# Attention and two MLPs in full precision: the ninth score block and its maxima, one bank for a head's sums, a 5/4 split of the subtraction, and new order numbers

## The chip, the cores and the metric

The kernel runs on one core of a Trainium2 chip. The metric is device time in microseconds (us) of one execution. TensorE (PE) multiplies, VectorE (DVE), ScalarE (ACT) and GpSimd (POOL) work elementwise, and SyncE (SP) issues all DMAs. Each of them works through its own list of instructions in order; they wait for each other on semaphores.

## The reference

Everything is fp32. Batch 2, 8 heads, 1152 keys, head size 64; two queries are averaged into one, so that each head has 576 queries. The attention output (1152 x 512) goes through two MLPs of width 2048.

```python
q_pool = q.reshape(B, H, S // 2, 2, D).mean(axis=3)
scores = scale * np.matmul(q_pool, k.transpose(0, 1, 3, 2))
scores = scores - np.max(scores, axis=-1, keepdims=True)
attn = np.exp(scores)
attn = attn / (np.sum(attn, axis=-1, keepdims=True) + 1e-09)
out = np.matmul(attn, v)
# x: the heads side by side, 1152 x 512
h = x @ w_in;  g = softplus(h);        x = g @ w_out      # first MLP
h = x @ w_in2; g = P(h) / (Q(h) + 1e-06); x = g @ w_out2  # second MLP, P and Q polynomials
```

## The kernel before

**What sets the order.** Nothing is issued where it is written. Each piece of work is an operation in a `Plan` (lines 62 to 194): its engine, a guessed duration, what it reads and writes, and a priority `at`. A list scheduler (`order`, line 130) then picks operation after operation by its guessed start times and by the priorities, gives out the buffers of the SBUF arena and of the eight PSUM banks, and the kernel issues the result (line 857). The priorities come from two tables of numbers, `OFF` for the attention and `OFF2` for the MLPs (lines 197 to 255), times a unit time T. The result is one fixed list for each engine. Which semaphore waits stand in it is decided afterwards by what the instructions touch.

**Attention, one head** (`head`, line 400). SP loads K, Q and V. POOL averages the query pairs (L423). PE transposes K and Q (L438, L450), ACT and DVE copy the transposes out of PSUM (L333 and L335 are the copy helper). A head is then worked off in two *units*, the two column halves of 288 queries (`hf` 0 and 1); 16 heads make 32 units, here numbered 0 to 31, so that even units are first halves. A score matrix stands with the keys on the partitions: nine blocks of 128 keys x 288 queries.

**One unit** (`unit`, line 471). PE computes the blocks in pairs into one of two PSUM buffers of two banks (L560, `sc`); block 8, which has no partner, is computed as two pieces of 144 columns, and it is the first of the unit (line 474). ACT copies each pair into the SBUF buffer `st` (L333, 128x576). DVE takes the running maximum over the blocks (L479): three operations over 576 columns with one input in PSUM, and two over 288 columns with both inputs in SBUF (lines 488 and 491: one brings in block 8 from `st`, one joins the two halves of the running maximum). PE transposes the maximum (L496), DVE reduces it (L500), PE spreads it over all partitions into a bank `mB` (L506), and ACT copies `mB` to SBUF (L512) for POOL. DVE subtracts the maximum from blocks 0 to 5 (L582, 128x1728, with `mB` in PSUM), POOL from blocks 6 to 8 (L582, 128x864, with the copy); ACT takes the exponential of each part (L589). The split is `ND = 6` (line 359).

**Values and sums** (`values`, line 517). PE multiplies the unit's nine blocks by V (L527, 64 rows, two blocks at a time in the two column halves of the array) and by a column of ones (L527, 1 row, four at a time in four quarters of the array) for the sums. Each unit has its own sum bank, its own copy of it by ACT (97x288) and its own four small DMAs (L545) that bring the four partial sums to 32 partitions. `norm` (line 595) adds them on POOL (L600, L603), takes the reciprocal on DVE (L605), sends it through DRAM (L607, L610) and multiplies on POOL (L616); each second head is then split into two fp32r parts `xh` and `xl` on POOL (L337, L348).

**The MLPs** (`moe`, line 645) multiply in fp32r, each product as three matmuls of high and low parts (L706, L788), with the weights converted by DVE (L664, L667, L670) and split by ACT and POOL. Some of the weight conversions stand between the attention's operations.

In the rows, `banks` is PSUM as a whole, `arena` and `arena_r` are the two large SBUF buffers.

Of the kernel before, what the change touches and what calls it, by code (L numbers as in the profile page):

```python
# [8 lines left out]
F32 = mybir.dt.float32  # L9
# [8 lines left out]
class Slot:  # L18


    def __init__(self, mem, off, size):
        self.mem, self.off, self.size = mem, off, size
        self.occ, self.over, self.lower = None, [], []

# [37 lines left out]
class Plan:  # L62
# [13 lines left out]
    def kind(self, name, phase, mem, offs, size, fifo=True):  # L76
        self.kinds[name] = Kind(name, phase, [Slot(mem, o, size) for o in offs], fifo)
# [52 lines left out]
    def order(self, slack, wait, stick):  # L130
        slots = [(kd, sl) for kd in self.kinds.values() for sl in kd.slots]
        for kd, sl in slots:
            for kx, x in slots:
                if x.mem is sl.mem and x.off < sl.off + sl.size and sl.off < x.off + x.size:
# [8 lines left out]
        while len(done) < len(self.ops):  # L143
            best = None
            for eng, l in cand.items():
# [15 lines left out]
                rank = lambda x: (x[1].prio + (abs(stick) if eng == "P" and x[1].mode != mode else 0.0), x[1].seq)  # L161
# [36 lines left out]
    'ld': 557.737,  # L198
    'tk': -3.506,
    'tke': -1199.93,  # L200
    'sq': 766.784,
    'tq': -1.626,
    'tqe': -1539.22,
    'lv': 734.191,
    'sc': -32.575,
    'ev': 2600.14,
    'mx': -558.886,
    'mt': -1059.58,
    'mr': -2884.99,
    'mb': -250.221,  # L210
    'sh': 2069.22,
    'ex': -278.049,
    'stick': 237.605,
    'ms': 872.18,
    'shg': 287.226,
    'exg': 898.812,
    'sm': 21.776,
    'so': -1632.41,
    'pv': 22.561,
    'pvs': -7.928,  # L220
    'po': -1438.22,
    'nm': 1549,
}
OFF2 = {
    'ld': -443.752,
    'hi': 746.06,
    'lo': -1233.92,
    'sp': 253.133,
    'ld2': -559.421,
    '1a': 1580.59,  # L230
    '1d': 171.246,
    '1y': 449.295,
    '1r': -443.221,
    '1z': -878.321,
    '1g': -600.605,
    'gh': 601.506,
    'gl': 330.365,
    '2h': -60.264,
    '2a': 372.297,
    '2t': -364.801,  # L240
    '2q': -994.888,
    '2b': 446.759,
    '2A': 737.678,
    '2m': 1387.29,
    '2n': 217.018,
    '2r': 386.142,
    '2g': -648.914,
    'out': 215.416,
    'end': 2687.08,
    'c1': -10155.3,  # L250
    'c2': -10450.6,
    'co': 13.248,
    's0': -557.188,
    's1': 1876.07,
# [7 lines left out]
WAIT = 0.088  # L262
SLACK = 0.009
# [27 lines left out]
def fused_kernel(  # L291
# [35 lines left out]
    ones = const.tile([128, 1], F32, name="ones")  # L327
# [31 lines left out]
    ND = 6  # L359
# [15 lines left out]
    def lay_ps(phase, **what):  # L375
        for name, (bs, n) in what.items():
# [5 lines left out]
             ("mp", 2, 2304), ("mb", 2, 1152), ("mc", 2, 32), ("dc", 2, 288), ("rc", 2, 72))  # L382
# [13 lines left out]
    def attention():  # L396
# [3 lines left out]
        def head(hd):  # L400
# [64 lines left out]
            dc = P.buf("dc", [32, 2, 4, HW // 32], F32)  # L465
            for hf in range(2):
                st = unit(hd, hf, kx, qT)
                values(hd, hf, st, vf, ud, dc, t0 + hf * T)
# [48 lines left out]
        def values(hd, hf, st, vf, ud, dc, t0):  # L517
            pv = P.buf("pv", [128, HW], F32)
            sm = P.buf("sm", [128, HW], F32)

            def tiles(out, lhs, m, c, n):
# [367 lines left out]
```

## Time and profile before

| | us |
|---|---|
| three runs: median (lowest to highest) | 730.65 (724.06 to 731.75) |
| the profiled execution, its own time | 729.63 |
| span of its instructions | 727.8 |

| engine | busy us | share of the span |
|---|---|---|
| PE | 682.6 | 94% |
| DVE | 582.3 | 80% |
| ACT | 540.5 | 74% |
| POOL | 505.2 | 69% |

The profile shows one execution. A group of instructions has a line of the kernel, an engine, what it writes and reads, and the mean of one in ns. Matmuls overlap, and their ends are modelled: a PE that reads as busy is not at its limit. The chain is the work that ended last, followed back from the end, so it tells which engine the time stood on.

### The profile page before, as it was taken

What the parts mean: (1) busy time and instruction counts of PE and PEld (TensorE: products, weight loads), DVE (VectorE), ACT (ScalarE), POOL (GpSimd) and SP (SyncE); (2) the same over time, 40 slices, a digit from 0 to 9 for tenths busy, and PEclk for the clock granted to TensorE, in tenths of its full rate; (3) what the DMA queues carried; (4) which work ended last, traced back from release to release, by engine and by line L of the source; (5) the groups of instructions that cost most, each with busy time, mean ns of one, the idle gap of its engine ahead of it and who ended that gap; (6) DMA issues with size and microseconds to landing.
All of it is one profiled execution on the core that took longest, in us unless ns stands there. A gap on an engine that the chain in (4) does not pass through costs nothing.

```text
span 727.8 us, 13061 instructions
## 1 busy us (share of the span) xinstructions
PE 682.6 (94%) x4612; PEld 530.4 (73%) x4612; DVE 582.3 (80%) x761; ACT 540.5 (74%) x1027; POOL 505.2 (69%) x513
## 2 busy tenths in 40 slices
PE   7998888879989889999999999999989999999997
PEld 5443444435444445569999999999978899898996
DVE  4787989767777789975325789999999988879796
ACT  3776677757767767796777887778887889986773
POOL 2443656444645554689767997879999889998673
PEclk9999999989999999999999999999999999999999
DMA  6222322212222224335102358788813011110011
GB/s 206 56 74 79 91 72 69 70 27 58 61 61 61 61 55 120 105 110 169 31 1 87 91 181 297 271 280 277 270 44 102 30 56 46 52 37 30 16 45 43
DMA packets 57457, 70.77 MB, mean 97 GB/s; under 512 B 13232, under 2 KB 38832, under 8 KB 57392
## 3 DMA queue, kind: packets, MB, share of 16 engines
q1 hardware_dynamic: 57392, 69.94, 31.4%
q8 instruction: 36, 0.59, 0.3%
q14 instruction: 29, 0.24, 0.1%
HBM read 58.99 MB, written 10.78 MB: 96 GB/s over the span
## 4 chain that ended last, share of the span: by engine, by line
PE 55%; DVE 19%; ACT 9%; POOL 6%; issue 5%; DMA 4%; SPq 1%; DVEq 0%; POOLq 0%; ACTq 0%
PE banks L706 21%; PE banks L788 20%; DVE arena L479 10%; PE banks L560 5%; PE banks L527 5%; ACT arena L333 4%; DVE arena L582 3%; ACT arena L589 1%; DVE banks L770 1%; POOL arena_r L348 1%; PE banks L496 1%; POOL arena L348 1%; DMA arena<-in_moe_w_out_dram 1%; POOL arena L766 1%; ACT arena_r L333 1%
## 5 line engine op out<-in xcount | busy, mean ns | idle before, releaser
L706 PE MATMUL banks<-xh,arena_r 128*128 128x384 f32 x768 | 212.3, 338 | 4.1 <-DVE arena_r L348 3.5
L788 PE MATMUL banks<-arena_r 128*128 128x384 f32 (+1 forms) x1008 | 214.0, 360 | 1.1 <-DVE arena_r L348 0.8
L333 ACT COPY arena<-banks 128x576 f32<-128x576 f32 (+5 forms) x309 | 147.2, 515 | 81.6 <-PE banks L560 35.1
L788 PEld LDWEIGHTS banks<-arena_r 128*128 128x128 f32 x1008 | 181.5, 188 | 16.2 <-POOL arena_r L348 1.3
L706 PEld LDWEIGHTS banks<-xh,arena_r 128*128 128x128 f32 x768 | 140.4, 188 | 10.5 <-DVE arena_r L348 7.4
L706 PE MATMUL banks<-xl,arena_r 128*128 128x384 f32 x384 | 129.3, 337 | 0.0
L770 DVE RECIPROCAL banks<-arena 128x384 f32<-128x384 f32 x48 | 122.6, 2554 | 6.7 <-POOL arena L762 5.4
L582 POOL TENSOR_TENSOR arena<-arena 128x864 f32<-128x864 f32 x32 | 65.8, 2057 | 82.8 <-ACT arena L333 82.7
L560 PE MATMUL banks<-arena 64*128 64x288 f32 (+1 forms) x640 | 104.3, 428 | 14.2 <-DVE arena L479 8.4
L348 POOL TENSOR_TENSOR arena<-arena 128x384 f32<-128x384 f32 x96 | 97.6, 1022 | 17.6 <-ACT arena L740 11.9
L348 POOL TENSOR_TENSOR arena_r<-arena,arena_r 128x512 fp32r<-128x512 f32 x64 | 82.5, 1299 | 18.8 <-ACT arena_r L333 18.6
L479 DVE TENSOR_TENSOR arena<-banks,arena 128x576 f32<-128x576 f32 x96 | 72.4, 754 | 28.2 <-ACT arena L333 23.3
L589 ACT ACTIVATE arena<-arena 128x864 f32<-128x864 f32 (+1 forms) x64 | 81.3, 1289 | 8.5 <-DVE arena L582 5.1
L560 PEld LDWEIGHTS banks<-arena 64*128 64x128 f32 x640 | 52.3, 191 | 45.4 <-DVE arena L479 15.3
L527 PE MATMUL banks<-arena 128*64 128x288 f32 (+1 forms) x640 | 83.8, 394 | 0.0
L348 DVE TENSOR_TENSOR arena_r<-banks,arena_r 128x384 fp32r<-128x384 f32 x96 | 52.8, 550 | 31.9 <-ACT arena_r L333 31.4
L706 PEld LDWEIGHTS banks<-xl,arena_r 128*128 128x128 f32 x384 | 72.1, 188 | 1.4
L333 ACT CAST arena_r<-banks 128x384 fp32r<-128x384 f32 x96 | 46.2, 481 | 26.1 <-DVE banks L771 12.1
L527 PEld LDWEIGHTS banks<-arena 128*64 128x64 f32 x640 | 40.7, 136 | 34.0 <-issue 10.2
L582 DVE TENSOR_TENSOR arena<-arena,banks 128x1728 f32<-128x1728 f32 x32 | 61.9, 1935 | 3.7 <-PE banks L506 2.9
L762 POOL TENSOR_TENSOR arena<-arena 128x384 f32<-128x384 f32 x48 | 49.0, 1021 | 22.3 <-ACT arena L756 22.1
L756 ACT ACTIVATE arena<-banks,par 128x384 f32<-128x384 f32 x96 | 63.8, 684 | 0.0
(54 smaller groups left out, 953.7 us busy)
## 6 DMA issues: line engine op xcount, KB each, us to landing
arena<-in_moe_w_in_dram SPq DMA_DIRECT2D x32, 512.0 KB, 4.3
arena<-in_moe_w_out_dram SPq DMA_DIRECT2D x32, 512.0 KB, 4.0
sp<-arena SPq DMA_DIRECT2D x32, 256.0 KB, 3.4
arena<-sp SPq DMA_DIRECT2D x32, 256.0 KB, 3.0
arena<-in_k_dram SPq DMA_DIRECT2D x16, 288.0 KB, 3.0
arena<-in_q_dram SPq DMA_DIRECT2D x16, 288.0 KB, 3.2
arena<-in_v_dram SPq DMA_DIRECT2D x16, 288.0 KB, 3.0
arena<-rr SPq DMA_DIRECT2D x16, 144.0 KB, 3.0
```

The source lines that it names most:

```text
L333: nc.scalar.copy(o, i)
L348: e.tensor_tensor(out=o, in0=a, in1=b, op=ALU.subtract)
L479: P.op("V", dve_t(m * HW), lambda: nc.vector.tensor_tensor(out=o(), in0=x(), in1=y(), op=ALU.max), r=r, w=w, at=t0 + (OFF['mx'] + 0.15 * j ...
L527: nc.tensor.matmul(out=out()[r:r + m, o:o + w], lhsT=lhs(x), rhs=st()[:, x, o:o + w], start=(c == 0), stop=(c == KC - 1), skip_group_check ...
L560: nc.tensor.matmul(out=ps()[:, i, 0:w], lhsT=kx()[D * i:D * i + D, j, :], rhs=qT()[D * i:D * i + D, q0:q0 + w], start=True, stop=True,)
L582: (nc.vector, nc.gpsimd)[g].tensor_tensor(out=s, in0=s, in1=mB()[:, None, :].to_broadcast([128, n, HW]), op=ALU.subtract)
L589: nc.scalar.activation(out=s, in_=s, func=AF.Exp, scale=escale)
L706: nc.tensor.matmul(out=hp(), lhsT=w()[:, kk * 128:(kk + 1) * 128], rhs=x[:, kk, :], start=(kk == 0 and n == 0), stop=(kk == KD - 1 and n = ...
L756: return lambda: nc.scalar.activation(out=o(), in_=i(), func=AF.Identity, scale=sc, bias=bi)
L762: P.op("G", pool_t(CW), lambda: nc.gpsimd.tensor_tensor(out=Q(), in0=t(), in1=ah(), op=ALU.add), r=[t, ah], w=[Q], at=a("2q"))
L770: P.op("V", (69 + 6.25 * CW) / 1e3, lambda: nc.vector.reciprocal(out=h(), in_=Q()), r=[Q], w=[h], at=a("2r"))
L788: nc.tensor.matmul(out=o()[:, 0:w_], lhsT=lt, rhs=rh, start=(f == 0 and n == 0), stop=(f == FG - 1 and n == 2),)
```

## The change

1. Block 8 is computed last in a unit instead of first. Its maximum is read from its PSUM bank: DVE takes the maximum of block 8's two pieces with one half of the running maximum, writes the result into free columns of block 8's own bank, and then joins that with the other half. Both operations over 288 columns now have one input in PSUM and one in SBUF.
2. `ND = 5`: DVE subtracts from five blocks (128x1440), POOL from four (128x1152); the two exponentials change with them.
3. The ones become two columns, 1 and 0 for the first unit of a head and 0 and 1 for the second, so that both units of a head accumulate into one bank, in two rows of each quarter. There is one copy of the sums per head (98x288) and four small DMAs per head instead of eight; the reciprocal is over 64x9 instead of 32x18.
4. The guessed overheads of the planner in the attention are raised (`extra`), and all numbers of `OFF` and `OFF2` are new, so that all lists are new. The values were on two column halves before and still are.

```diff
-        self.extra = {"A": 0.05, "V": 0.04, "G": 0.03, "P": 0.01}
+        self.extra = {"A": 0.1, "V": 0.075, "G": 0.09, "P": 0.01}
...
-    'ld': 557.737,
+    'ld': 845.214,
...
-    ND = 6
+    ND = 5
...
-            scores(st, kx, qT, hf, KC // 2, t0)
...
-            for j in range(KC // 2):
+            for j in range((KC + 1) // 2):
                 ps = scores(st, kx, qT, hf, j, t0)
                 x = lambda ps=ps: ps()[:, :, 0:HW]
                 if j == 1:
                     top(mp, x, lambda: st()[:, 0:2, :], 2, j, [ps, (st, 0), (st, 1)], [mp])
-                    half = lambda: mp()[:, 0, :]
-                    top(half, half, lambda: st()[:, KC - 1, :], 1, j, [(st, KC - 1), mp], [mp])
+                elif j == KC // 2:
+                    two = lambda a: a.rearrange("p (a b) -> p a b", a=2)
+                    half = lambda ps=ps: ps()[:, 0, HW // 2:HW // 2 + HW]
+                    top(lambda: two(half()), lambda ps=ps: ps()[:, :, 0:HW // 2], lambda: two(mp()[:, 0, :]), 1, j,
+                        [ps, mp], [(ps, 1)])
+                    top(mx, half, lambda: mp()[:, 1, :], 1, j, [(ps, 1), mp], [mx])
                 elif j:
                     top(mp, x, mp, 2, j, [ps], [mp])
-            top(mx, lambda: mp()[:, 0, :], lambda: mp()[:, 1, :], 1, KC // 2, [mp], [mx])
...
-                                              (4, sm, lambda c: ones, 1, 3, 'sm')):
+                                              (4, sm, lambda c: ones[:, 2 * hf:2 * hf + 2], 2, 3, 'sm')):
...
+            if hf == 0:
+                return
+            sd = P.buf("sd", [128, HW], F32)
+            P.op("A", act_t(HW), lambda: cp("A", sd()[0:98, :], sm()[0:98, :]), r=[sm], w=[sd], at=t0 + OFF['so'] * T)
```

What the new numbers do to the lists is seen in three places.

**DVE in the middle of the attention.** Before, from the first maximum of unit 22 (an even unit) to the first of unit 23. L479 is the running maximum, L335 a copy of transposed K or Q, L605 the reciprocal, L582 the subtraction, L500 the reduction, L540 a sum of values:

```order
L479 TENSOR_TENSOR arena<-banks,arena 128x576
L335 COPY arena<-banks 128x256
L479 TENSOR_TENSOR arena<-arena 128x288
L479 TENSOR_TENSOR arena<-banks,arena 128x576 x2
L335 COPY arena<-banks 128x288
L479 TENSOR_TENSOR arena<-arena 128x288
L605 RECIPROCAL arena<-arena 32x18
L582 TENSOR_TENSOR arena<-arena,banks 128x1728
L500 TENSOR_REDUCE arena<-banks 96x3
L540 TENSOR_TENSOR arena<-banks,arena 64x288
L582 TENSOR_TENSOR arena<-arena,banks 128x1728
L479 TENSOR_TENSOR arena<-banks,arena 128x576
```

Now, from the first maximum of unit 20 (also even) over the first of unit 21 to unit 20's own subtraction; the lines are 5 to 7 higher (L484 maximum, L589 subtraction, L340 copy, L546 sum of values, L508 reduction, L612 reciprocal):

```order
L484 TENSOR_TENSOR arena<-banks,arena 128x576
L589 TENSOR_TENSOR arena<-arena,banks 128x1440
L340 COPY arena<-banks 128x288
L484 TENSOR_TENSOR arena<-banks,arena 128x576 x2
L484 TENSOR_TENSOR banks<-banks,arena 128x288
L484 TENSOR_TENSOR arena<-banks,arena 128x288
L546 TENSOR_TENSOR arena<-banks,arena 64x288
L508 TENSOR_REDUCE arena<-banks 96x3
L484 TENSOR_TENSOR arena<-banks,arena 128x576
L612 RECIPROCAL arena<-arena 64x9
L484 TENSOR_TENSOR arena<-banks,arena 128x576
L589 TENSOR_TENSOR arena<-arena,banks 128x1440
```

The two operations over 288 columns now stand together at the end of the unit's maxima, and they touch `banks`. The subtraction of unit 19 has moved in behind unit 20's first maximum, and that of unit 20 stands between the maxima of unit 21.

**ACT at the same place.** Before, from the copy of the spread maximum of unit 22, over the exponentials of unit 22, to the first copies of unit 24 (576 columns: a pair of blocks; 128x288: `mB`, a transposed Q or block 8; 128x384: transposed K; 97x288: sums; 64x288: values):

```order
L333 COPY arena<-banks 128x288
L333 COPY arena<-banks 128x576
L333 COPY arena<-banks 128x288
L589 ACTIVATE arena<-arena 128x1728
L589 ACTIVATE arena<-arena 128x864
L333 COPY arena<-banks 64x288
L333 COPY arena<-banks 128x576
L333 COPY arena<-banks 128x384
L333 COPY arena<-banks 128x576
L333 COPY arena<-banks 97x288
L333 COPY arena<-banks 128x288
L333 COPY arena<-banks 128x576 x2
```

Now, from the copies of the second and third pair of blocks of unit 20, over the exponentials of unit 19, to the copies of block 8 of unit 20 and of a transposed Q (one row), the first three pairs of unit 21, K, the spread maximum of unit 20 and the last pair of unit 21:

```order
L338 COPY arena<-banks 128x576 x2
L338 COPY arena<-banks 98x288
L596 ACTIVATE arena<-arena 128x1440
L596 ACTIVATE arena<-arena 128x1152
L338 COPY arena<-banks 64x288
L338 COPY arena<-banks 128x288 x2
L338 COPY arena<-banks 128x576 x3
L338 COPY arena<-banks 128x384
L338 COPY arena<-banks 128x288
L338 COPY arena<-banks 128x576
```

The copy of block 8, which stood ahead of a unit's pairs (the row 128x288 ahead of 128x576 x2), now follows them and, in an even unit, stands behind both exponentials of the unit before and a copy of values. The copy of an even unit's spread maximum stands ahead of the last pair of the next unit.

**SP at the start of the program.** Before:

```order
L410 DMA arena<-in_k_dram 128x576
L412 DMA arena<-in_k_dram 128x64
L414 DMA arena<-in_q_dram 96x6x128
L410 DMA arena<-in_k_dram 128x576
L412 DMA arena<-in_k_dram 128x64
L462 DMA arena<-in_v_dram 128x576 x2
```

Now:

```order
L467 DMA arena<-in_v_dram 128x576 x2
L415 DMA arena<-in_k_dram 128x576
L417 DMA arena<-in_k_dram 128x64
L419 DMA arena<-in_q_dram 96x6x128
L415 DMA arena<-in_k_dram 128x576
```

The two loads of V, which are needed last in a head, have moved ahead of the first K and Q.

## Rows read from the trace of the kernel before

**Rows 1.** Stretches: us, PE, PEld, DVE, ACT, POOL busy, PE clock, DMA share, GB/s

```profile
20.00:129.40 109.40, 96.58 (x845) 50.41 (x847) 94.93 (x127) 78.89 (x132) 54.87 (x49) 0.98 0.27 74
129.40:172.91 43.51, 37.31 (x311) 19.44 (x311) 29.15 (x41) 28.51 (x47) 20.62 (x19) 0.92 0.19 51
172.91:206.13 33.22, 30.77 (x275) 16.19 (x279) 27.33 (x38) 23.69 (x41) 16.96 (x17) 1.00 0.23 58
206.13:261.59 55.46, 49.61 (x457) 26.48 (x453) 43.59 (x59) 39.23 (x67) 28.17 (x25) 1.00 0.22 54
225.10:242.62 17.52, 17.09 (x163) 8.92 (x155) 13.16 (x21) 13.41 (x23) 11.54 (x11) 1.00 0.26 62
129.40:309.24 179.84, 161.56 (x1435) 86.73 (x1435) 141.85 (x194) 127.23 (x212) 93.62 (x88) 0.98 0.25 68
340.00:520.00 180.00, 179.58 (x1026) 178.63 (x1025) 130.89 (x217) 140.63 (x304) 151.18 (x168) 1.00 0.54 177
560.00:700.00 140.00, 139.89 (x707) 126.55 (x706) 122.92 (x113) 114.25 (x224) 118.69 (x116) 1.00 0.12 38
```

**Rows 2.** The maximum's two forms: duration ns min/median/max, first and last start

```profile
L479 DVE TENSOR_TENSOR arena<-banks,arena x96: 682/758/776, 11.9 to 303.3; 128x576 f32<-128x576 f32 x96
L479 DVE TENSOR_TENSOR arena<-arena x64: 395/460/3546, 13.2 to 304.5; 128x288 f32<-128x288 f32 x64
```

**Rows 3.** Instructions in order of time, POOL and DVE: start us, us, idle before

```profile
218.41 2.02 POOL L582 TENSOR_TENSOR arena<-arena 128x864 f32<-128x864 f32 x1 [3.26 <-ACT arena L333]
...
219.07 1.68 DVE L479 TENSOR_TENSOR arena<-arena 128x288 f32<-128x288 f32 x1
...
222.75 0.45 DVE L479 TENSOR_TENSOR arena<-arena 128x288 f32<-128x288 f32 x1
```

**Rows 4.** Groups by line and shape: busy us, mean ns, idle before

```profile
L348 POOL TENSOR_TENSOR arena<-arena 128x384 f32<-128x384 f32 x96 | 97.6, 1022 | 17.6 <-ACT arena L740 11.9 <-ACT arena L735 2.6 <-DVE arena L605 0.5
L479 DVE TENSOR_TENSOR arena<-banks,arena 128x576 f32<-128x576 f32 x96 | 72.4, 754 | 28.2 <-ACT arena L333 23.3 <-PE banks L560 1.2
L582 POOL TENSOR_TENSOR arena<-arena 128x864 f32<-128x864 f32 x32 | 65.8, 2057 | 82.8 <-ACT arena L333 82.7
L582 DVE TENSOR_TENSOR arena<-arena,banks 128x1728 f32<-128x1728 f32 x32 | 61.9, 1935 | 3.7 <-PE banks L506 2.9 <-ACT arena L333 0.8
L479 DVE TENSOR_TENSOR arena<-arena 128x288 f32<-128x288 f32 x64 | 57.2, 894 | 1.1
L589 ACT ACTIVATE arena<-arena 128x1728 f32<-128x1728 f32 x32 | 52.9, 1652 | 5.2 <-DVE arena L582 5.1
L589 ACT ACTIVATE arena<-arena 128x864 f32<-128x864 f32 x32 | 29.6, 926 | 3.3 <-POOL arena L582 3.3
L540 DVE TENSOR_TENSOR arena<-banks,arena 64x288 f32<-64x288 f32 x32 | 14.1, 442 | 5.9 <-ACT arena L333 5.7
L333 ACT COPY arena<-banks 97x288 f32<-97x288 f32 x32 | 12.8, 400 | 3.3 <-PE banks L527 2.0 <-ACT arena L333 0.5
L605 DVE RECIPROCAL arena<-arena 32x18 f32<-32x18 f32 x16 | 4.0, 247 | 1.6 <-POOL arena L603 1.4
```

**Rows 5.** The chain that ended last, in order of time: start us, us, what

```profile
214.18 1.30 DVE arena L479
215.48 0.14 issue
215.61 0.50 PE banks L496 x3
216.12 0.71 PE banks L560 x4
216.83 0.02 issue
216.85 1.19 ACT arena L333 x2
218.04 0.02 issue
218.06 0.76 DVE arena L479
```

**Rows 6.** Waits: us in total, times, longest us

```profile
POOL arena L616 <- DMA arena<-rr: 12.9, 5, 5.7
```

**Rows 7.** DMA issues: KB each, median us from issue to landing

```profile
arena<-in_v_dram SPq DMA_DIRECT2D x16, 288.0 KB, 3.0
arena<-rr SPq DMA_DIRECT2D x16, 144.0 KB, 3.0
...
rr<-arena SPq DMA_DIRECT2D x16, 2.2 KB, 1.4
```

**Rows 8.** The start in order of time, SP and DVE

```profile
3.15 0.91 SPq L462 DMA_DIRECT2D arena<-in_v_dram  x2
...
6.07 0.95 DVE L423 TENSOR_TENSOR arena<-arena 96x768 f32<-96x768 f32 x1 [4.49 <-DMA arena<-in_q_dram]
```

More of the change, by code (lines that the diff above doesn't have):

```diff
@@ L18, with __init__, hits @@
 class Slot:
-    def __init__(self, mem, off, size):
+    def __init__(self, mem, off, size, parts=None):
         self.mem, self.off, self.size = mem, off, size
+        self.parts = parts or [(off, size)]
         self.occ, self.over, self.lower = None, [], []
+    def hits(self, x):
+        return self.mem is x.mem and any(a < c + d and c < a + b for a, b in self.parts for c, d in x.parts)
 class Kind:
@@ L130, in order @@
     def order(self, slack, wait, stick):
+        slack, wait, stick = abs(slack), abs(wait), abs(stick)
         slots = [(kd, sl) for kd in self.kinds.values() for sl in kd.slots]
@@ L133, in order @@
             for kx, x in slots:
-                if x.mem is sl.mem and x.off < sl.off + sl.size and sl.off < x.off + x.size:
+                if sl.hits(x):
                     sl.over.append(x)
@@ L197 @@
 OFF = {
-    'ld': 557.737,
[L199 to L222, printed above, removed]
+    'wait': 9.522,
+    'slack': -13.871,
+    'ld': 845.214,
+    'tk': -1.558,
+    'tke': 455.339,
+    'sq': 170.768,
+    'tq': -2.117,
+    'tqe': -1513.99,
+    'lv': 169.897,
+    'sc': -281.419,
+    'ev': 834.657,
+    'mx': 68.852,
+    'mt': -1960.16,
+    'mr': -636.184,
+    'mb': -1524.95,
+    'sh': 4714.6,
+    'ex': 1562.13,
+    'stick': 2124.22,
+    'ms': 459.13,
+    'shg': 1637.44,
+    'exg': 1969.44,
+    'sm': 65.9,
+    'so': -4395.44,
+    'pv': 61.789,
+    'pvs': -20.29,
+    'po': -2549.06,
+    'nm': 3824.62,
 }
 OFF2 = {
[L225 to L254, printed above, removed]
+    'ld': -339.463,
+    'hi': -4407.94,
+    'lo': -737.322,
+    'sp': 294.491,
+    'ld2': -176.92,
+    '1a': 3630.63,
+    '1d': 2000.53,
+    '1y': -1669.07,
+    '1r': -1003.45,
+    '1z': -931.452,
+    '1g': 405.722,
+    'gh': -322.945,
+    'gl': 257.971,
+    '2h': -2608.64,
+    '2a': -907.365,
+    '2t': -1616.68,
+    '2q': 1050.43,
+    '2b': -419.031,
+    '2A': 93.019,
+    '2m': 1378.43,
+    '2n': -0.808,
+    '2r': 961.146,
+    '2g': 242.058,
+    'out': 767.634,
+    'end': 4941.37,
+    'c1': -13083.6,
+    'c2': -2071.71,
+    'co': 5.118,
+    's0': -3.69,
+    's1': 96.708,
 }
@@ L464, in head @@
             ud = P.buf("ud", [64, SQ], F32)
-            dc = P.buf("dc", [32, 2, 4, HW // 32], F32)
+            dc = P.buf("dc", [64, 4, HW // 32], F32)
+            sm = P.buf("sm", [128, HW], F32)
             for hf in range(2):
                 st = unit(hd, hf, kx, qT)
-                values(hd, hf, st, vf, ud, dc, t0 + hf * T)
+                values(hd, hf, st, vf, ud, sm, dc, t0 + hf * T)
             norm(hd, ud, dc, t0)
@@ L515, in unit, with values, tiles @@
             return st
-        def values(hd, hf, st, vf, ud, dc, t0):
+        def values(hd, hf, st, vf, ud, sm, dc, t0):
             pv = P.buf("pv", [128, HW], F32)
-            sm = P.buf("sm", [128, HW], F32)
-            def tiles(out, lhs, m, c, n):
+            def tiles(out, lhs, m, c, n, first, last):
                 w = HW if c + n <= KC - 1 else HW // n
@@ L527, in tiles @@
                     nc.tensor.matmul(out=out()[r:r + m, o:o + w], lhsT=lhs(x), rhs=st()[:, x, o:o + w],
-                                     start=(c == 0), stop=(c == KC - 1), skip_group_check=True)
+                                     start=(c == 0 and first), stop=(c == KC - 1 and last), skip_group_check=True)
             for n, out, lhs, m, mode, key in ((2, pv, lambda c: vf()[:, c, :], D, 2, 'pv'),
-                                              (4, sm, lambda c: ones, 1, 3, 'sm')):
+                                              (4, sm, lambda c: ones[:, 2 * hf:2 * hf + 2], 2, 3, 'sm')):
                 for c in range(0, KC, n):
                     full = c + n <= KC - 1
-                    P.op("P", 0.484 if full else 0.49 / n, lambda a=(out, lhs, m, c, n): tiles(*a),
-                         r=([vf] if m > 1 else []) + [(st, c + i) for i in range(n if full else 1)], w=[out],
+                    P.op("P", 0.484 if full else 0.49 / n, lambda a=(out, lhs, m, c, n, m > 2 or hf == 0, m > 2 or hf == 1): tiles(*a),
+                         r=([vf] if m > 2 else []) + [(st, c + i) for i in range(n if full else 1)], w=[out],
                          at=t0 + (OFF[key] + OFF['pvs'] * c) * T, mode=mode)
             uh = P.buf("uh", [64, HW], F32)
-            sd = P.buf("sd", [128, HW], F32)
             P.op("A", act_t(HW), lambda: cp("A", uh(), pv()[D:2 * D, :]), r=[pv], w=[uh], at=t0 + OFF['po'] * T)
@@ L552, in scores @@
             pair = 2 * j + 1 < KC
-            if not pair:
-                at = t0 + OFF['sc'] * T - 0.01
             w = HW if pair else HW // 2
@@ L856, in fused_kernel @@
             moe()
-        for o in P.order(SLACK, WAIT, OFF['stick']):
+        for o in P.order(0.01 * OFF['slack'], 0.01 * OFF['wait'], OFF['stick']):
             o.fn()
```

32 lines of the change are left out of this document (15 added, 17 removed).

## The prediction

> **What bounds the kernel now.** I read the stretches first [rows 1]. In the MLPs PE has no room: 179.58 busy of 180.00 us in the first, 139.89 of 140.00 in the second. Their matmuls are not touched and only their order is new, so what is won must be won in the attention. There no engine is full: from the reduction of unit 0 (at 20.00) to that of unit 31 (at 309.24) lie 109.40 + 179.84 = 289.24 us for 31 units, or 15.5 heads: 18.66 us per head. DVE is busy for 94.93 + 141.85 of them, 82%.
>
> So I read the chain next. Over one head it goes round all engines, and most often through DVE: a maximum of 1.30 us, PE's transposes, a pair of blocks, two copies by ACT, the next maximum [rows 5]. The 1.30 is one of the maxima over 288 columns with both inputs in SBUF, half the columns of the others. The view of this line has 64 of them, with a minimum of 395 ns, a median of 460 and a maximum of 3546 [rows 2]; their mean is 894, more than the 754 of a maximum over 576 columns out of PSUM [rows 4]. The time order shows why: one starts at 219.07 while POOL's subtraction runs from 218.41 to 220.43, and takes 1.68 us, until 0.3 behind POOL's end; another at 222.75, with POOL idle, takes 0.45 [rows 3]. These maxima wait for POOL.
>
> **The change part by part.** *Maxima from PSUM.* One input and for one of the two the result too move to PSUM. The nearest row is the sum of values, one input in PSUM, 288 columns: 442 ns [rows 4]; that is the unhindered SBUF form within 20 ns. I take 0.46, so DVE spends 64 x (0.894 - 0.46) = 27.8 us less. The bounds: nothing, if PSUM operands wait in the same way, against which stands that of the 96 maxima over 576 columns, with one input in PSUM, none took over 776 ns [rows 2]; and all 27.8.
>
> *Split 5/4.* For DVE, two rows over 1728 and 576 columns give (1935 - 754)/1152 = 1.025 ns per column, so 1440 columns take 1.64 us, 0.295 less, 9.4 us over 32. For POOL (2057 - 1022)/(864 - 384) = 2.156 ns per column, so 1152 columns take 2.68, 0.62 more. The exponentials: (1652 - 926)/864 = 0.840 per column, 1.41 and 1.17, together unchanged [rows 4].
>
> *One sum bank per head.* 16 copies of 0.40 by ACT go, 6.4 us, and 64 small DMAs. Neither is on the chain that I walk below; the sums' matmuls stay as many. I cost this at nothing. Its cover is ACT's slack, 127.23 busy of 179.84 [rows 1]; without it the 6.4 would be won.
>
> *New lists.* Here the gain can be lost again, so I walked one head of the new lists, with even unit 20 and odd unit 21 as example, from the end of DVE's subtraction for unit 20. The waits are those that follow from what an instruction reads, from the lists, and from one thing that the trace shows: DVE's maximum over a pair waits for ACT's copy of the same pair, although both only read it; 23.3 of the 28.2 us of idle time ahead of these maxima are put down to that copy [rows 4]. The walk, in us:
> - ACT copies the spread maximum, 0.40; POOL subtracts for unit 20, 2.68; ACT takes that exponential, 1.17, then a copy of values, 0.40, then the first two pairs of the next even unit, 1.19 for two [rows 5]: 5.84.
> - DVE: that unit's first maximum, 0.75, then the subtraction of unit 21 that stands behind it, 1.64: 2.39, in all 8.23.
> - ACT: both exponentials of unit 21, 1.41 + 1.17 (POOL's share is ready by then), a copy of values, 0.40, and only now the copy of the even unit's block 8, 0.40: 3.38, in all 11.61.
> - DVE: the second maximum over 288, 0.46. PE: transposes 0.50, the next unit's second pair 0.71 [rows 5]. ACT: its copy, 0.60. In all 13.88.
> - DVE: first maximum 0.75, reciprocal 0.25, second maximum 0.75, subtraction 1.64: 3.39, in all 17.27, and the round is closed.
>
> About eight hand-overs come on top, 0.02 from ACT to DVE and 0.14 from DVE to PE [rows 5]: 0.16 to 1.1, and I take 0.4. So **17.7 us per head**, against 18.66. DVE's wait for POOL is gone from the round, but POOL's subtraction (0.62 longer), both exponentials and a wait for ACT stand in it. That wait is new: the even unit's second small maximum waits for ACT's copy of block 8 out of the same bank, and the copy stands behind two exponentials. Behind it wait, on DVE, a sum of values and the reduction, and on PE the transposes. Were the copy not awaited, DVE would get there 2.6 after the subtraction of unit 21 (a copy, 0.44, two maxima, 1.50, the first small one, 0.46, hand-overs) instead of 3.4: some 0.75 per head, 12 us over 15.5 heads, and the sum below would be 705.
>
> The Trainium skill (PSUM — Partial Sum Buffer, section on PSUM bank collisions) says that any two engines on one bank and one group of 32 partitions must be kept apart by semaphores, two readers included. By that rule the wait stays, as in the walk, and the sum is 717 rather than 705; the waits of the pair maxima for ACT agree.
>
> *The start.* SP now issues two loads of V ahead of the first K and Q. They take 0.91 us to issue [rows 8], so Q lands at least that much later, and DVE starts on Q at 6.07 as soon as it lands. From above I bound it by the 3.0 us that such a load takes from issue to landing [rows 7], as if K and Q had to wait for all of it, and take 2.0.
>
> *The MLPs.* Same matmuls on a full PE: nothing to win but 0.4 us of 180 [rows 1], at most a few us to lose where an order is worse, since in the second MLP DVE is at 122.92 and POOL at 118.69 of 140. I take 0; the bounds are -1 and +6.
>
> **The sum.** 15.5 heads x (18.66 - 17.7) = 14.9 less, 2.0 more: 12.9 less than the profiled execution's 729.63, which is 716.7. That execution is 1.0 under the median of the runs shown; I predict 717.
>
> **The rivals.** *A: all of the waiting comes off.* If the round holds more slack than my walk has, DVE's whole saving counts: 27.8 + 9.4 = 37.2, less 2.0 at the start: 729.6 - 35.2 = 694. For it: DVE is the most frequent engine of the chain, and in the old lists two heads ran at 33.22/2 = 16.6 us each between 172.91 and 206.13 [rows 1], so shorter rounds exist. Against it: the new wait for ACT. Chance 0.15.
>
> The Trainium skill (SBUF — State Buffer, section on who interferes with whom) says that a DVE instruction with two SBUF inputs and a GpSimd instruction that reads SBUF exclude each other for their whole length, and that with at most one SBUF input there is no such contention. By it the 27.8 us vanish entirely, which only bears on DVE's own time; the trace agrees in the direction that it shows, DVE behind POOL.
>
> *B: the round is set elsewhere and nothing measurable changes.* PE's matmuls are as many as before, and between 225.10 and 242.62 PE is busy for 17.09 of 17.52 us [rows 1]. If that is nearly its need, or if hand-overs are at their upper bound, a head takes 18.4 to 18.5: 15.5 x 0.2 = 3 less, 2 more, some 728. Against it: a busy PE here includes modelled ends. The split adds to it: POOL's 0.62 is on the round. Chance 0.20.
>
> *C: slower, by POOL's wait for a DMA.* POOL's new list has subtraction 20, the multiplication of an earlier head (L616 before), subtraction 21 in a row. The multiplication waits for the reciprocals to come back from DRAM. From the small reciprocal to the end of POOL's subtraction 20 the walk gives 0.75 + 1.64 + 0.40 + 2.68 and hand-overs, 5.7 us; the way through DRAM is 1.4 + 3.0 = 4.4 [rows 7] and SP has two loads of K between the two, which wait for PE. Some 1 us is left, and about 1 more until subtraction 21 is due. What comes later than these 2 us is paid by every head, since that subtraction feeds the exponential ahead of block 8's copy. Slower by over 1% means 21 us or 1.4 per head, so the way would have to take some 7.8 us. POOL did wait so before, 12.9 us in 5 times, the longest 5.7 [rows 6]. At 1.5 per head the time is 717 + 23 = 740. Chance 0.13.
>
> **How the numbers follow.** My forecast has 0.52; its own range goes by the hand-overs and the MLPs, 17.4 to 18.1 per head: 708 to 726. The range to hold the time 8 times in 10 reaches into A, to 697, and over B, to 735, and leaves out half of A and C. About 1%, 7.3 us, is what a measurement of this kernel can tell from no change; 723.3 is the border. Of my forecast nearly all lies below it: faster 0.65, within 1% 0.22, slower 0.13.
>
> **What would show it.** The two maxima over 288 columns at 0.44 to 0.48 us, none over 0.6: if their mean stays near 0.9, the first step is wrong. DVE's subtraction at 1.64, POOL's at 2.68. A period of 17.4 to 18.0 us from an even unit's reduction to the next in the middle of the attention, with DVE's idle time ahead of the second small maximum put down to ACT. The chain there should run through POOL's subtraction and ACT's exponentials more than before. The first DVE work on Q at about 8. If the period is under 17 the wait for ACT isn't paid, and A holds; if POOL's largest wait is for the reciprocals' DMA in most heads, C; if PE shows no gaps over 0.5, B. A loss of PE's busy share in the MLPs would make me wrong from the side that I left at nothing.

## The result, and the profile after

| | us |
|---|---|
| before, four runs beside those of the change: median | 731.2 |
| after, four runs: median (lowest to highest) | 709.25 (708.72 to 712.22) |
| ratio after / before | 0.973, 95% interval 0.966 to 0.980 |
| the profiled execution of after, and its span | 708.75; 706.9 |

The kernel is 22 us faster by the medians, 21 by the two profiled executions (729.63 before). The forecast was 717, and 12.9 less from one profiled execution to the other. The time lies inside the range given.

The stretches of after, as in [rows 1]: us, then PE, PEld, DVE, ACT and POOL busy, PE clock, DMA share, GB/s. The first two are bounded by the reductions of units 0, 14 and 31, the third lies in the MLPs.

```profile
20.59:135.11 114.52, 108.01 (x966) 56.79 (x968) 90.04 (x145) 89.22 (x148) 70.96 (x55) 1.00 0.28 78
135.11:290.81 155.70, 143.33 (x1304) 76.46 (x1305) 108.85 (x173) 111.34 (x181) 89.42 (x85) 1.00 0.25 70
340.00:520.00 180.00, 180.00 (x1024) 178.63 (x1024) 142.53 (x221) 145.75 (x311) 154.97 (x167) 1.00 0.55 179
```

The MLPs still run on a full PE, the attention does not. I put unit times side by side, always from the start of one unit's reduction on DVE to that of another (L500 before, L508 after):

| us | before | after | difference |
|---|---|---|---|
| start to unit 0 | 19.99 | 20.59 | +0.6 |
| units 0 to 14 (7 heads) | 130.12 | 114.52 | -15.6 |
| units 14 to 20 (3 heads) | 56.02 | 54.97 | -1.1 |
| units 20 to 26 (3 heads) | 55.46 | 54.65 | -0.8 |
| units 26 to 31 | 47.65 | 46.08 | -1.6 |
| unit 31 to the end | 418.52 | 416.13 | -2.4 |

So three quarters of the gain lie in the first seven heads. From unit 14 to 26 the heads follow a fixed pattern, and there a head went from 18.6 to 18.3 in the mean; most periods from one even unit to the next are 18.1 in after. The stretches of before held some half clock: 0.98 of the full 2.4 GHz in 109.40 us and 0.92 in 43.51 [rows 1], which is 4.4 and 7.0 us at 1.2 GHz; after has 1.00 in both. At most half of such time is lost, so 5.7 us of the gain at the most; the units 14 to 20, which hold some of it, took only 0.6 more than the like units 20 to 26.

What the line of the running maximum shows in after (min/median/max of the durations in ns), against [rows 2]:

```profile
L484 DVE TENSOR_TENSOR arena<-banks,arena x128: 433/756/759, 14.0 to 286.2; 128x576 f32<-128x576 f32 x96, 128x288 f32<-128x288 f32 x32
L484 DVE TENSOR_TENSOR banks<-banks,arena x32: 447/464/467, 17.4 to 285.7; 128x288 f32<-128x288 f32 x32
```

No small maximum takes more than 467 ns (the 32 in the first row at most 458), where one took 3546 before. That it was POOL can be read off the trace of before: 31 of its 64 small maxima took over 470 ns, and each of the 31 ended 0.30 to 0.32 us behind the end of an instruction of POOL; none of the other 33 took over 460. The groups by line and shape, as in [rows 4]:

```profile
L484 DVE TENSOR_TENSOR banks<-banks,arena 128x288 f32<-128x288 f32 x32 | 14.8, 461 | 8.3 <-PE banks L567 6.5 <-ACT arena L338 1.1
L484 DVE TENSOR_TENSOR arena<-banks,arena 128x288 f32<-128x288 f32 x32 | 14.6, 455 | 5.0 <-ACT arena L338 4.4
L589 DVE TENSOR_TENSOR arena<-arena,banks 128x1440 f32<-128x1440 f32 x32 | 52.7, 1646 | 0.6 <-PE banks L514 0.4 <-ACT arena L338 0.2
L589 POOL TENSOR_TENSOR arena<-arena 128x1152 f32<-128x1152 f32 x32 | 84.8, 2649 | 58.9 <-ACT arena L338 57.5 <-DMA arena<-arena 1.3
L596 ACT ACTIVATE arena<-arena 128x1440 f32<-128x1440 f32 x32 | 45.3, 1417 | 0.8 <-DVE arena L589 0.8
L596 ACT ACTIVATE arena<-arena 128x1152 f32<-128x1152 f32 x32 | 37.4, 1167 | 7.8 <-POOL arena L589 7.8
L338 ACT COPY arena<-banks 98x288 f32<-98x288 f32 x16 | 6.4, 401 | 1.2 <-PE banks L534 0.5
```

All prices of the forecast hold within 2%. The waits (us in total, times, longest):

```profile
POOL arena L589 <- ACT arena L338: 57.5, 24, 5.9
DVE arena L484 <- ACT arena L338: 39.9, 52, 1.9
ACT arena L338 <- DVE arena L589: 24.7, 12, 2.6
POOL arena L623 <- DMA arena<-rr: 8.4, 9, 1.7
```

The third row has no price in my walk, which begins with it: ACT's copy follows the end of DVE's subtraction. ACT was idle for up to 2.6 us before that, 24.7 us in all. Last, the chain of waits over one regular head, from one subtraction to the next of the same kind (start us, us, what):

```profile
193.36 1.57 DVE arena L589
194.93 0.02 issue
194.95 0.41 ACT arena L338
195.36 0.07 issue
195.43 2.65 POOL arena L589
...
199.72 1.19 ACT arena L338 x2
200.91 0.02 issue
200.94 0.77 DVE arena L484
201.70 0.04 issue
201.75 0.76 PE banks L567 x4
202.50 3.06 PE banks L534 x36
205.56 0.93 PE banks L567 x8
206.49 0.40 PE banks L455 x3
206.89 1.08 PE banks L534 x16
207.97 0.46 PE banks L504 x3
208.43 0.71 PE banks L567 x4
209.14 0.02 issue
209.16 0.65 ACT arena L338
...
211.46 1.57 DVE arena L589
```

The first half is the walk of the prediction: subtraction, copy, POOL, exponential, copies, maximum. In the second half the walk had DVE's subtraction, two exponentials, the copy of block 8 and the join; here the chain stays on PE from 201.75 to 209.14. PE isn't busy all the time: between 190 and 244 us its gaps of over 0.3 us are three in each head, of 0.32, 0.44 and 0.58 us, all three ended by a maximum of DVE.

### The profile page after: what moved, and what is told of

The parts are those of the page before. It is cut to its first block, busy times and chain, and to the rows that moved or that the text cites. A ratio compares the mean times of both kernels' runs of the same rounds, so it can differ in the third digit from the quotient of the medians.

```text
span 706.9 us, 12922 instructions
## 1 busy us (share of the span) xinstructions
PE 676.8 (96%) x4612; PEld 527.5 (75%) x4612; DVE 546.1 (77%) x762; ACT 536.4 (76%) x1011; POOL 519.0 (73%) x513
## 4 chain that ended last, share of the span: by engine, by line
PE 66%; DVE 11%; ACT 10%; POOL 6%; issue 5%; DMA 1%; SPq 0%; ACTq 0%; POOLq 0%; DVEq 0%
PE banks L713 24%; PE banks L795 21%; PE banks L534 11%; PE banks L567 7%; ACT arena L338 5%; DVE arena L484 4%; DVE arena L589 3%; POOL arena L589 3%; ACT arena L763 2%; DVE banks L777 2%; PE banks L504 1%; POOL arena L769 1%; POOL arena_r L353 1%; PE banks L455 1%; POOL arena L773 1%
## 5 line engine op out<-in xcount | busy, mean ns | idle before, releaser
L338 ACT COPY arena<-banks 128x576 f32<-128x576 f32 (+5 forms) x293 | 141.2, 522 | 71.9 <-DVE arena L589 24.7
L589 POOL TENSOR_TENSOR arena<-arena 128x1152 f32<-128x1152 f32 x32 | 84.8, 2649 | 58.9 <-ACT arena L338 57.5
L484 DVE TENSOR_TENSOR arena<-banks,arena 128x576 f32<-128x576 f32 (+1 forms) x128 | 87.0, 680 | 43.6 <-ACT arena L338 39.9
L567 PE MATMUL banks<-arena 64*128 64x288 f32 (+1 forms) x640 | 105.6, 425 | 14.9 <-DVE arena L484 12.2
L596 ACT ACTIVATE arena<-arena 128x1440 f32<-128x1440 f32 (+1 forms) x64 | 81.9, 1292 | 8.6 <-POOL arena L589 7.8
L567 PEld LDWEIGHTS banks<-arena 64*128 64x128 f32 x640 | 50.3, 187 | 48.1 <-DVE arena L484 26.4
L534 PE MATMUL banks<-arena 128*64 128x288 f32 (+1 forms) x640 | 79.9, 389 | 0.6 <-ACT arena L596 0.6
L338 ACT CAST arena_r<-banks 128x384 fp32r<-128x384 f32 x96 | 46.1, 481 | 26.7 <-DVE banks L778 14.4
L589 DVE TENSOR_TENSOR arena<-arena,banks 128x1440 f32<-128x1440 f32 x32 | 52.7, 1646 | 0.6 <-PE banks L514 0.4
```

The lines of the kernel that those rows point to most:

```text
L338: nc.scalar.copy(o, i)
L484: P.op("V", dve_t(m * HW), lambda: nc.vector.tensor_tensor(out=o(), in0=x(), in1=y(), op=ALU.max), r=r, w=w, at=t0 + (OFF['mx'] + 0.15 * j ...
L534: nc.tensor.matmul(out=out()[r:r + m, o:o + w], lhsT=lhs(x), rhs=st()[:, x, o:o + w], start=(c == 0 and first), stop=(c == KC - 1 and last ...
L567: nc.tensor.matmul(out=ps()[:, i, 0:w], lhsT=kx()[D * i:D * i + D, j, :], rhs=qT()[D * i:D * i + D, q0:q0 + w], start=True, stop=True,)
L589: (nc.vector, nc.gpsimd)[g].tensor_tensor(out=s, in0=s, in1=mB()[:, None, :].to_broadcast([128, n, HW]), op=ALU.subtract)
L596: nc.scalar.activation(out=s, in_=s, func=AF.Exp, scale=escale)
```

## The experiments

The theory: what pays is that DVE no longer waits for POOL in the small maxima, and a regular head is a round through ACT's copy of the spread maximum, POOL and ACT's exponentials. Rivals: the new lists or the one sum bank bring the gain; the join's wait for ACT's copy of block 8 holds part of it back; the regular heads are set by PE. All ratios are to the kernel before on the same chip, with 95% intervals.

### Only the maxima (e1)

```diff
-                    top(half, half, lambda: st()[:, KC - 1, :], 1, j, [(st, KC - 1), mp], [mp])
+                    top(half, half, spread, 1, j, [(st, KC - 1), mp], [mp])
...
-            top(mx, lambda: mp()[:, 0, :], lambda: mp()[:, 1, :], 1, KC // 2, [mp], [mx])
+            top(mx, lambda: mp()[:, 0, :], spread, 1, KC // 2, [mp], [mx])
```

`spread` is 288 columns of the PSUM bank of the spread maximum, so that block 8 and half of the running maximum are left out of the maximum; the lists are those of before.

> The kernel before with its lists unchanged; only the second input of the two maxima over 288 columns comes from PSUM (the bank of the unit before's spread maximum) instead of SBUF, so the maximum leaves out block 8 and half of the running maximum. If DVE's waits for POOL were what the change takes away, these 64 maxima fall from a mean of 894 ns to 450 to 470, none over 0.6 us, and the time falls by 12 to 25 us, most of it before 160 us, where the longest waits stood (two of over 3 us). If the old lists close the gap again (rival B), the 64 still fall to 0.46 but the time falls by less than 4 us.

Measured: 707.56 us, ratio 0.976 (0.971 to 0.980). The line of the maximum:

```profile
L480 DVE TENSOR_TENSOR arena<-arena,banks x64: 381/453/455, 12.7 to 285.0; 128x288 f32<-128x288 f32 x64
```

64 operations, none above 455 ns, 445 in the mean. Ahead of them DVE was idle for 1.1 us in all before [rows 4], so their own length is what went. One operand moved to PSUM, in unchanged lists, brings as much as the whole change (0.973, and 0.977 in the repetition below). It comes at other places: units 0 to 14 take 122.08 (-8.0), 14 to 31 148.24 (-10.9), not most of it before 160 us as expected, and the heads from 20 to 26 take 16.84 each. So beside this step the new lists, the split and the one sum bank together add nothing that can be told from none; the sum bank was not tried alone.

### Half of it taken back (e7)

```diff
-                    top(lambda: two(half()), lambda ps=ps: ps()[:, :, 0:HW // 2], lambda: two(mp()[:, 0, :]), 1, j,
+                    top(lambda: two(mp()[:, 0, :]), lambda ps=ps: ps()[:, :, 0:HW // 2], lambda: two(mp()[:, 0, :]), 1, j,
...
-                    top(mx, half, lambda: mp()[:, 1, :], 1, j, [(ps, 1), mp], [mx])
+                    top(mx, lambda: mp()[:, 0, :], lambda: mp()[:, 1, :], 1, j, [(ps, 1), mp], [mx])
```

> The changed kernel, same lists; block 8's maximum goes back to SBUF instead of to PSUM, so that the second of the two, the join, has both inputs in SBUF again (and no longer touches block 8's bank). Lock theory: an even unit's join starts where POOL adds query pairs (1.8 us) and an odd one's while POOL subtracts, so joins take 1 to 2.2 us in the regular heads and the time rises by 12 to 25 us. Rival, that the wait for ACT out of the same bank costs as much as the lock: the time stays within 4 us.

Measured: 717.16 us, 0.989 (0.983 to 0.994). The join by shape:

```profile
L484 DVE TENSOR_TENSOR arena<-arena 128x288 f32<-128x288 f32 x32 | 32.1, 1003 | 0.8
```

With both inputs in SBUF again its mean is back at 1003 ns, 17.5 us over 32, and the time rises by 8 us against the repetition of after (0.977), less than the 12 to 25 expected. Of that 6.5 lie in units 0 to 14 (121.03); units 20 to 26 take 54.65, exactly as after. But the joins are not equally long in the two stretches, first units 0 to 14, then 20 to 26:

```profile
L484 DVE TENSOR_TENSOR arena<-arena 128x288 f32<-128x288 f32 x14 | 18.3, 1306 | 0.3
L484 DVE TENSOR_TENSOR arena<-arena 128x288 f32<-128x288 f32 x6 | 4.3, 718 | 0.2
```

In the first heads DVE's small maxima take 11.9 us more than in after, and 6.5 us are lost: DVE's time counts there, but not in full. In the regular heads only the odd unit's join grew, from 0.46 to 0.98 us, and the even unit's no longer waits 0.47 us for ACT. That half a microsecond per head is free there; more was not put to the test.

### The join's wait for ACT (e3)

```diff
-                "p (a b) -> p a b", a=2), ps()[:, :, 0:w]),
+                "p (a b) -> p a b", a=2), ps()[:, :, 0:w] if pair else st()[:, 2 * j - 1, :].rearrange("p (a b) -> p a b", a=2)),
```

ACT's copy of block 8 reads the copy of another block instead of the bank that the join uses, so the join need not wait for it; block 8 is left out of the exponentials.

> The changed kernel, same lists; ACT's copy of block 8 reads block 7 from SBUF instead of block 8 from its bank (block 8's scores are left out of the exponentials), so ACT does the same work and the join no longer waits for it. By the walk on record the wait is on the round at 0.75 us a head: 12 us less. By what the changed kernel's trace shows, PE is still busy with values, block 8 and sums when the join ends (207.45 against a start of the transposes at 207.90), so the wait is hidden: 0 to 3 us less.

Measured: 711.3 us, 0.980 (0.976 to 0.985). The join's idle time fell from 5.0 us, 4.4 of them put down to ACT, to 0.8. Units 0 to 14 take 114.22, a regular head 18.10: nothing moved. (The 2.2 us that this execution takes beyond that of after lie before unit 0, where it ran 13.7 us at half clock.) The 0.75 per head that the prediction put on this wait isn't there.

### The split (e2)

```diff
+            d0, m = ((0, 6), (6, 3))[g]
...
-                s = st()[:, c0:c0 + n, :]
+                s = st()[:, d0:d0 + m, :]
```

The lists are those of after; subtractions and exponentials go back to six blocks and three.

> The changed kernel, same lists; only the sizes of the subtraction and the exponentials go back to 6 and 3 blocks. By the round as the trace of the changed kernel shows it (DVE's subtraction once, POOL's once, POOL's exponential once): 0.30 more, 0.59 and 0.24 less, so 0.5 a head or 8 us less than the changed kernel. Rival A's view, that DVE's own time is what counts: 9.4 us of DVE time more, so 3 to 9 us more.

Measured: 713.38 us, 0.984 (0.979 to 0.989). A regular head takes 17.68, 0.42 less, so POOL's subtraction is on the round there. The first seven heads take 121.09 against 114.52, and it isn't faster in all. Its trace has half clock at two places there (49.7 and 121.3 us, 3.4 us each), of which after has none; that explains at most 3.4 of the 6.6. DVE's longer subtraction, 0.30 us in each of 14 units, is 4.2 us; the same edit in e10 below, with no half clock there, costs 3.2 in these units (113.72 against 110.48 in e8).

### The change again, and code and numbers crossed (a0, e4, e5)

e4 is the changed code with the numbers and overheads of before, e5 the code of before with the new ones. The lists of each were never made for it.

> The changed kernel once more, beside the runs of this call, so that differences of 1% can be read on one chip. A ratio of 0.966 to 0.980 to the kernel before, as first measured.

> The changed code (maxima from PSUM, block 8 last, 5/4 split, one sum bank) with the old order numbers and overheads. If the maxima out of PSUM are the whole gain, as the kernel before with only those suggests (ratio 0.976), this is within 1% of the changed kernel: 0.965 to 0.985. If the new numbers are needed for the changed code, it is above 0.985.

> The kernel before with the new order numbers and overheads alone; block 8 first, small maxima in SBUF, 6/3, two sum banks. Lock theory: the 64 maxima still wait for POOL (mean 0.8 to 1.0 us) and the ratio is 0.99 to 1.02. If the new lists are what gains, it is under 0.985.

Measured: the change again 709.01 us, 0.977 (0.972 to 0.983); e4 752.91, 1.036 (1.030 to 1.042); e5 745.84, 1.026 (1.019 to 1.032). Both crossings are slower than before. In e4 units 0 to 14 take 144.13 us, 29.6 more than in after. A row of its stretches:

```profile
16.00:100.00 84.00, 60.94 (x455) 31.84 (x453) 49.23 (x76) 43.15 (x70) 35.75 (x30) 0.78 0.23 68
```

PE is busy for 61 of 84 us, and the granted clock has a mean of 0.78; 37 us of these 84 are at 1.2 GHz, 29 of them behind the reduction of unit 0, so that half clock explains at most half of the 29.6. PE's gaps and the half clock stand together here; the run doesn't show which brings the other. In e5 the small maxima have a mean of 875 ns, close to before. What the numbers are worth can't be told apart from the code that they were made for.

### ACT's copy ahead of DVE's subtraction (e8)

Both read the same bank `mB`. In after DVE's subtraction often comes first in the order of issue, and ACT waits for its end (12 times). Here the copy comes first wherever it stood behind; each engine's own list stays the same, only who waits for whom changes. `tag` marks the two operations of a unit.

```diff
-        for o in P.order(0.01 * OFF['slack'], 0.01 * OFF['wait'], OFF['stick']):
+        done = P.order(0.01 * OFF['slack'], 0.01 * OFF['wait'], OFF['stick'])
+        for sb in [o for o in done if o.tag and o.tag[0] == "sub"]:
+            cb = next(x for x in done if x.tag == ("copy",) + sb.tag[1:])
...
+                    done.remove(cb)
+                    done.insert(i0, cb)
...
+        for o in done:
```

> The changed kernel with the same list on every engine; only where DVE's subtraction and ACT's copy of the same spread maximum touch one bank, the copy now goes first in all units (in the changed kernel, in even units of the regular heads, the copy waits for the subtraction). ACT is idle there (it waited 24.7 us in 12 waits for DVE's subtraction), and POOL's subtraction starts some 2.5 us earlier. Theory of the round (subtraction, copy, POOL, exponential, copies, maximum, PE): the regular heads fall from 18.1 us to 16.8 to 17.4 and the time by 6 to 14 us. Rival, that PE's list is the round's floor: the heads stay at 18.0 or above, the time within 3 us.

> e8 once more, unchanged, on the chip of e9, e10 and e11, so that these are compared on one chip: 0.955 to 0.965 of the kernel before, regular heads 16.5 us.

Measured: 697.47 us, 0.960 (0.954 to 0.965), 11.5 less than the change on the same chip; on another chip 695.89, 0.960 (0.955 to 0.964). The time order of after at one such place (start us, us, idle before):

```profile
193.28 1.64 DVE L589 TENSOR_TENSOR arena<-arena,banks 128x1440 f32<-128x1440 f32 x1
...
194.95 1.24 ACT L338 COPY arena<-banks 128x288 f32<-128x288 f32 x3 [2.57 <-DVE arena L589]
195.43 2.64 POOL L589 TENSOR_TENSOR arena<-arena 128x1152 f32<-128x1152 f32 x1 [4.33 <-ACT arena L338]
```

The same place in the second run of e8, where the copy is one of ACT's four from 181.19 on:

```profile
183.25 2.65 POOL L590 TENSOR_TENSOR arena<-arena 128x1152 f32<-128x1152 f32 x1 [1.66 <-ACT arena L339]
183.39 1.65 DVE L590 TENSOR_TENSOR arena<-arena,banks 128x1440 f32<-128x1440 f32 x1
```

POOL and DVE now subtract side by side, where POOL started 2.15 behind DVE. Units 20 to 26 fall from 54.65 to 49.44, 16.5 a head, and 0 to 14 to 110.48. On one chip (first run of e8, repetition of after) units 0 to 31 are 14.4 us shorter, 255.79 against 270.21, and what follows is 1.2 longer. Waits and stretch of the second run:

```profile
POOL arena L590 <- ACT arena L339: 31.8, 17, 5.9
POOL arena L624 <- DMA arena<-rr: 26.0, 10, 5.3
```

```profile
190.00:244.00 54.00, 52.88 (x499) 28.69 (x500) 40.04 (x64) 42.52 (x68) 33.17 (x30) 1.00 0.21 59
```

POOL's wait for the copy is nearly halved, its wait for the reciprocals (rival C's) has trebled, and PE is busy for 52.88 of 54.00 us, against 49.49 at the same times in after. Of its three gaps per head one is left, of 0.32 us.

### Three tests on that (e9, e10, e11)

e9 is e1 with the copy first, e10 is e8 with the 6/3 split of e2, e11 is e8 with the two V loads behind the first loads of K and Q:

```diff
+        dma = [o for o in done if o.eng == "S"]
+        for ld in dma[:2]:
+            done.remove(ld)
+            done.insert(done.index(dma[6]) + 1, ld)
```

> The kernel before with its old order of work, the second input of the small maxima read from PSUM (as in e1), and in addition ScalarE's copy of the half's maximum ahead of VectorE's subtraction wherever it stood behind it. As in e1, block 8 and half of the running maximum are left out of the stabilising maximum. Theory that the wait of the copy on VectorE's subtraction sits on the round only where a GpSimd subtraction of the same unit starts from that copy: here the exps that follow wait for both subtractions, so a regular head gains between 0 and 0.5 us on e1's 16.84, at most 8 us in all; I expect 0 to 6 us less than e1's ratio gives (e1 was 0.976 of before, so 702 to 708 beside a before of 725). Rival, that the copy-first gain of e8 (11.5 us) comes from the reordering as such: the same 11 to 12 us here, 696.

> e8 (the changed kernel with ScalarE's copy ahead of VectorE's subtraction) with the 6/3 split of the subtraction and the exps in place of 5/4. Theory that in e8 TensorE's own list sets the regular heads (16.5 us a head): a shorter GpSimd subtraction then gives nothing, the total stays within 3 us of e8 and the regular heads stay within 0.15 us of 16.5. Rival, that the round through GpSimd's subtraction still sets them: 0.4 us less a head as in e2, 6 us less in all.

> e8 with the V loads of the first two heads issued behind the first K and Q loads. Theory that the loads of V ahead of them delay the first work on Q from 6.07 us (before) to 8.37 us (after): the first VectorE work on Q returns to 6.1 to 7.1 us and the total falls by 1 to 2.5 us against e8. Rival, that the start is hidden by work that comes later: no change (within 0.7 us), with the first reduction of unit 0 earlier but the reduction of unit 14 where it was.

Measured: e9 707.58 us, 0.976 (0.971 to 0.981), the same as e1. POOL's wait for the copies fell from 70.9 to 58.3 us, and a regular head takes 17.05 instead of 16.84. In e1 ACT had waited for DVE's subtraction for 9.2 us only, in 8 waits, against 24.7 in after; now DVE's subtraction waits for the copy:

```profile
DVE arena L584 <- ACT arena L334: 13.6, 12, 1.9
```

In e1 that was 1.3 us, in e8 it is 4.7. So in the old lists the edit moves a wait more than it takes one away. e10 697.18, 0.962 (0.957 to 0.967), 1.3 us more than e8 beside it, 49.24 for units 20 to 26: a shorter POOL no longer helps. e11 696.29, 0.960 (0.954 to 0.965), 0.4 more than e8. The first DVE work on Q, in e11, in e8 beside it, and in after:

```profile
7.17 0.94 DVE L429 TENSOR_TENSOR arena<-arena 96x768 f32<-96x768 f32 x1
```

```profile
7.94 0.94 DVE L429 TENSOR_TENSOR arena<-arena 96x768 f32<-96x768 f32 x1
```

```profile
8.03 0.42 DVE L340 COPY arena<-banks 128x256 f32<-128x256 f32 x1 [6.31 <-PE banks L443]
8.37 0.94 DVE L428 TENSOR_TENSOR arena<-arena 96x768 f32<-96x768 f32 x1
```

It came 0.8 earlier than in e8, but the nine executions that load V first lie anywhere from 6.98 to 8.63 (the four with the old order of loads from 5.78 to 6.60), and the total didn't fall: the rival holds. In the new list DVE first copies the transposed K, so there the start hangs on K, not on Q alone.

## Why the prediction was right or wrong

**Maxima from PSUM: right in price and in weight.** 0.46 was said, 0.461 and 0.455 measured. The Trainium skill (SBUF — State Buffer, section on who interferes with whom) has a DVE operation with two SBUF inputs and one of GpSimd that reads SBUF exclude each other. e1 and e7 agree: means of 445 against 894 and of 455 against 1003 ns by the place of the inputs. What the prediction didn't see is that this step alone, in the old lists, brings as much as the whole change (e1).

**Split: right in its prices.** 1.646, 2.649, 1.417 and 1.167 against 1.64, 2.68, 1.41 and 1.17. The sum bank, put at nothing, was not tried alone; no run shows its worth.

**New lists, the walk: the failed step.** 17.7 us per head were said for all 15.5 heads. The regular ones take 18.1 to 18.3, just outside the 17.4 to 18.0 that the prediction named as its sign; the gain there is 0.3 to 0.4 and not 0.96, and the first seven heads gain 2.2 each. The sum of 14.9 for the attention came near the 19.0 measured (289.24 to 270.22) because the two errors pull against each other: that the time lies in the range is in part luck.
- In the regular heads, the sub-step "both exponentials of unit 21, a copy of values, the copy of block 8, then the join" is not what sets the second half. From the end of the first maximum (201.70) PE needs 6.27 us until the transposes of the next maximum (207.97), with sums, values and scores in its list; the walk's way through DVE and ACT takes 5.6 (1.64, 3.38, 0.46 and hand-overs), and the join did end before that, at 207.45. So the wait that I called new and priced at 0.75 per head exists, with 0.47 us of idle time in an even unit, but is covered by PE, and e3 shows nothing for its removal. The Trainium skill (PSUM — Partial Sum Buffer, section on PSUM bank collisions) says that two engines on one bank and one group of 32 partitions have to be kept apart, two readers included. The trace agrees, with 4.4 us of waits in after and none left in e3's 0.8. That the wait costs something was my step.
- The first half of the walk is right: e2 shortens POOL's subtraction and the head falls by 0.42. Where I let ACT's copy follow the end of DVE's subtraction I took the order as given; e8 shows that this order of two readers, which nothing in the computation asks for, costs 11.5 us in these lists.
- In the first seven heads I had no walk at all and applied the mean. DVE spends 2 x 0.894 + 1.935 = 3.72 us per unit on small maxima and subtraction before [rows 4], and 0.461 + 0.455 + 1.646 = 2.56 now; 14 units x 1.16 = 16.3, and 15.6 came off. There rival A's arithmetic comes near, but not because DVE's time counts in full: e7 put 11.9 us back on DVE and lost 6.5, and some of the 15.6 can be the clock of before. What the new lists gave there beside it is not shown. From unit 14 on the same 1.16 per unit is 19.7, and 3.4 came off. That is near rival B's figure (a head at 18.1 to 18.3, B had 18.4 to 18.5), but PE isn't the floor there: it has a gap of 0.58 us in each head, and in e8 the head falls to 16.5.

**The start: mis-sized.** 2.0 were said, 0.6 came; the repetition of after even has its first reduction at 19.68, 0.3 before that of before. The first work on Q at 8.37 was as forecast (about 8), but before had half clock from 14.8 on, and the first unit's reduction hardly moved. e11 finds nothing to win there.

**The MLPs: near.** Nothing was said, with at most 1 to win; from unit 31 to the end it is 2.4 less, 1.8 in the repetition. That stretch also holds the end of the attention, and no run splits the two.

**Rival C fell** for the change (8.4 us, longest 1.7). In e8, with shorter heads, the wait returns with 26.0 us while the time falls.

Left open: what sets the first seven heads, where DVE's time counts but not in full, and whether PE's list is what holds the old lists in e9: PE is busy for 52.63 of 54.00 us there between 190 and 244, and for 53.25 in e1, which speaks for it, but no run tests it.

## What to carry to other kernels

Where a DVE operation's maximum duration is many times its minimum, look for POOL working at the same moment, and move one of its inputs to PSUM: 64 operands of 288 columns were worth 17 us here, without a new order. Where two engines read one PSUM bank, look whether one waits for the other's end, as ACT's copy did here for DVE's subtraction, and try the short reader on whom a slow engine waits in front (11.5 us here, nothing in another order of work). A mean over all rounds of a loop is no round: walk an early and a regular one, and close the walk over PE's list too.

## What the runs showed of the hardware

- A DVE maximum over 288 columns with two SBUF inputs took up to 3546 ns before and 1003 in the mean in e7, against at most 467 with one input in PSUM, also with the result written to PSUM. Each of the 31 in before and of the 18 in e7 that took over 470 ns ended 0.30 to 0.32 us behind an instruction of POOL.
- ACT's copy of 0.41 us waited in 12 places of after for the end of DVE's subtraction of 1.65 us, though both only read the bank; ACT was idle for up to 2.6 us before it.
- The granted clock fell to half in stretches of 3.4 to 17 us that differ between executions of like kernels: none in after from 13.8 us until its end, one of 6.8 us in one run of e8 and one of 3.4 at another place in the other; in e4, with PE idle for 23 of the first 84 us from 16 on, 37 us in all.
